# A gated linear recurrence taken in steps of 64 tokens in place of 128, ahead of two expert layers

## The chip, the cores and the metric

The kernel runs on one core of one Trainium2 chip. The metric is device time in microseconds (us), the median of several executions. A profile is one execution taken by the hardware profiler, and its times run from the start of its span. The engines are PE (TensorE, the matrix engine; its weight loads are listed apart as PEld and overlap the matmuls), DVE (VectorE), ACT (ScalarE), POOL (GpSimd) and SP (SyncE, which issues the transfers here).

## What is computed

A recurrence over 768 tokens for 4 batches of 8 heads with 48 features each, then two layers of the same size on its 3072 tokens by 384 features:

```python
def _attn_ref(q, k, v, f_logit):
    f = 1.0 / (1.0 + np.exp(-f_logit))
    state = np.zeros((B, H, D, D), dtype=np.float32)
    for t in range(S):
        state = f[:, :, t, :, None] * state + np.einsum('bhd,bhe->bhde', k[:, :, t], v[:, :, t])
        y[:, :, t] = np.einsum('bhd,bhde->bhe', q[:, :, t], state)
    return y

x = y.transpose(0, 2, 1, 3).reshape(B * S, H * D)
h = x @ w_in;  x = (h * clip(h + 3, 0, 6) / 6) @ w_out           # 384 -> 2048 -> 384
h = x @ w_in2; x = (h * tanh(log1p(exp(h)))) @ w_out2            # 384 -> 2048 -> 384
```

## The kernel before

**The recurrence in units.** A unit u is 128 tokens (C) of one batch, all 8 heads; there are 24, six to a batch, so units 0, 6, 12 and 18 begin a batch (`first`) and units 5, 11, 17 and 23 end one (`last`). Heads lie in four pairs p, two heads on 112 of the 128 rows (rows 0 to 47 and 64 to 111). `attention` (line 231) does for each unit: DVE bounds f (L245), ACT takes exp and log, DVE sums the logs along the tokens with one scan (L251; a `cap` tile with a zero at the first token of each pair starts each sum anew), ACT takes two exponentials, and DVE multiplies k and q by them (L201), so that the decay inside a unit has become a scale of each token. On PE then stand five pieces, all in f32: `scores` (L262), q times k for 128 by 128 tokens into two banks; `turn` (L281), four transposes of k, copied by ACT to `kn`; `outer` (L288), k outer v, which is what the unit adds to the state; and `values` (L302), q times the old state `sd` and then the masked scores A times v. DVE masks the two banks of scores (L271), adds the outer products to the state `st` and scales it (`carry`, L322 and L323), ACT copies the state into the two diagonal blocks of `sd` for the next unit, and ACT and DVE take the result apart into a high and a low half, `xh` and `xl` (L182, L198), which the layers multiply. A unit that ends a batch has no `turn`, `outer` and `carry`; one that begins a batch has no product with the state.

**The array in tiles.** A matmul that uses few rows or columns of the array is placed on a part of it, and parts work at the same time: in `scores` a matmul uses 48 rows and 128 columns (two parts), in `outer` 128 rows and 64 columns (two parts), in `values` 128 rows and 32 columns (four parts). An f32 matmul stands in the trace as two records, each with a weight load of its own; one of the layers' matmuls (f32r) is one record.

**The layers.** The weights of each layer stand in 16 slices f. The tokens go in blocks (384 or 512 tokens, the last of 256), seven to each layer. For each f of each block `hidden` (line 342) issues nine matmuls into a bank h (three parts of the features, times xh·wh, xl·wh, xh·wl), ACT and DVE form g and its halves gh and gl, and nine more matmuls add to three banks o. The first layer's weights are taken apart into `wh` and `wl` while block 0 runs: a transfer `raw`, two steps on ACT, two on DVE (L215, L217), one more of each (L182, L198).

**What sets the order.** `Plan` holds every operation with an engine, an estimated cost, the keys that it reads and writes, and a rank, and `emit` (line 110) lays the program out as a list scheduler: an engine that comes free takes the ready operation of the lowest rank. Every engine then runs its list in that order and waits where something isn't there. Units 0 to 3 stand at the head with ranks 1.1 apart (HEAD_GAP), ahead of block 0; the later ones are spread over the f of the block before theirs. Before rank 1, where PE would idle by the plan, `warm` puts filler matmuls on the tile `cap`, up to 30 us by the plan.

## Time and profile before

| what | us |
| --- | --- |
| median of 3 executions (lowest, highest) | 927.75 (927.59, 930.64) |
| the profiled execution itself | 927.91 |
| its span | 926.1 |
| PE busy | 907.6 (98%) |
| DVE busy | 673.6 (73%) |
| ACT busy | 571.2 (62%) |

The span is 1.8 us shorter than the time of the same execution. The three stretches that matter below are the head (0 to 34 us, units 0 to 3 and the first weights), block 0 (34 to 124.5 us) and all behind it. A row of instructions says at which us the first of a group began, how long the group took to its end (ends overlap, so paces are read from one start to the next), the engine, the line, the operation, what it writes and reads, and in brackets what the engine waited for.

### The profile page before, as it was taken

To read this page: it belongs to the slowest core of one execution; us is meant where nothing else is said; L and a number is where in the kernel's file an instruction comes from. 1 tells how busy PE (TensorE), PEld (TensorE's weight loads), DVE (VectorE), ACT (ScalarE), POOL (GpSimd) and SP (SyncE) were. 2 spreads that over 40 slices of the span, in tenths; PEclk is the share of its full clock that TensorE was granted. 3 is DMA by queue.
4 is the path that set the end of the run, shared out by engine and by line. 5 is a ranking of instruction groups with operands and counts; after the bars stand their busy time and mean duration, and the time that the engine had idled before them with its cause. 6 is when DMAs were issued, how large, how long until landed. Compare 5 with 4: busy or idle time off the path is not lost.

```text
span 926.1 us, 15491 instructions
## 1 busy us (share of the span) xinstructions
PE 907.6 (98%) x6173; PEld 799.3 (86%) x6173; DVE 673.6 (73%) x1127; ACT 571.2 (62%) x1022; POOL 0.2 (0%) x4
## 2 busy tenths in 40 slices
PE   9999899999999999999999999999999999999996
PEld 8777689999999988888899988888888888999996
DVE  7999876776555644453355887978878878888895
ACT  7889866666554544343255765766666666676674
POOL 0000000000000000000000000000000000000000
PEclk9999999999999999999999999999999999999998
DMA  9665466665321311110033300200100101000000
GB/s 275 214 211 179 156 218 209 197 216 195 114 65 52 99 42 42 43 46 2 1 103 120 126 21 0 69 1 8 56 0 18 43 1 33 23 7 27 1 27 21
DMA packets 33488, 75.92 MB, mean 82 GB/s; under 512 B 3840, under 2 KB 11008, under 8 KB 33408
## 3 DMA queue, kind: packets, MB, share of 16 engines
q1 hardware_dynamic: 33408, 74.86, 25.1%
q8 instruction: 50, 0.82, 0.4%
q14 instruction: 30, 0.25, 0.1%
HBM read 59.11 MB, written 15.73 MB: 81 GB/s over the span
## 4 chain that ended last, share of the span: by engine, by line
PE 84%; DVE 7%; DMA 3%; ACT 3%; issue 2%; SPq 0%; DVEq 0%; ACTq 0%
PE o L195 40%; PE h L195 26%; PE a L195 13%; PE m L195 5%; DMA raw<-w 2%; DVE we L215 1%; DVE we L217 1%; DVE wl L198 1%; DMA o<-ft 1%; DVE A L271 1%; DVE g L370 1%; ACT f L182 1%; DVE q L201 0%; PE m L283 0%; DMA f<-ft 0%
## 5 line engine op out<-in xcount | busy, mean ns | idle before, releaser
L195 PE MATMUL o<-gh,wh 128*128 128x512 f32 (+2 forms) x666 | 242.2, 364 | 0.0
L195 PE MATMUL o<-gh,wl 128*128 128x512 f32 (+2 forms) x666 | 239.3, 359 | 0.0
L195 PE MATMUL o<-gl,wh 128*128 128x512 f32 (+2 forms) x666 | 239.2, 359 | 0.0
L195 PE MATMUL h<-xh,wh 128*128 128x384 f32 (+2 forms) x471 | 172.1, 365 | 1.1 <-ACT wh L182 0.8
L195 PE MATMUL h<-xh,wl 128*128 128x384 f32 (+2 forms) x471 | 169.7, 360 | 2.5 <-DVE wl L198 2.5
L195 PE MATMUL h<-xl,wh 128*128 128x384 f32 (+2 forms) x471 | 169.0, 359 | 0.3 <-DVE xl L198 0.3
L195 PEld LDWEIGHTS o<-gh,wh 128*128 128x128 f32 x666 | 125.2, 188 | 17.1 <-issue 2.4
L370 DVE SCALAR_TENSOR_TENSOR g<-g,h 128x384 f32<-128x384 f32 (+1 forms) x112 | 68.1, 608 | 97.6 <-ACT g L182 97.6
L195 PEld LDWEIGHTS o<-gh,wl 128*128 128x128 f32 x666 | 125.2, 188 | 13.2
L195 PEld LDWEIGHTS o<-gl,wh 128*128 128x128 f32 x666 | 125.3, 188 | 13.0 <-DVE gl L198 0.2
L182 ACT ACTIVATE g<-h,small 128x384 f32<-128x384 f32 (+1 forms) x112 | 69.7, 623 | 92.8 <-PE h L195 72.5
L182 ACT ACTIVATE gh<-q 128x512 fp32r<-128x512 f32 (+2 forms) x110 | 63.0, 573 | 86.5 <-DVE q L201 81.3
L195 PEld LDWEIGHTS h<-xh,wl 128*128 128x128 f32 x471 | 88.5, 188 | 14.3 <-DVE wl L198 5.5
L195 PEld LDWEIGHTS h<-xh,wh 128*128 128x128 f32 x471 | 88.5, 188 | 13.5 <-ACT wh L182 3.0
L182 ACT ACTIVATE gh<-g 128x384 fp32r<-128x384 f32 (+1 forms) x112 | 63.4, 566 | 56.6 <-DVE g L370 56.2
L195 PEld LDWEIGHTS h<-xl,wh 128*128 128x128 f32 x471 | 88.5, 188 | 8.9 <-DVE xl L198 0.7
L198 DVE TENSOR_TENSOR gl<-g,gh 128x384 fp32r<-128x384 f32 (+1 forms) x112 | 68.4, 611 | 35.7 <-ACT gh L182 35.6
L182 ACT ACTIVATE q<-k,small 128x512 f32<-128x512 f32 (+2 forms) x112 | 73.7, 658 | 14.4 <-DVE k L378 14.1
L201 DVE TENSOR_TENSOR q<-q,k 128x512 f32<-128x512 f32 (+2 forms) x112 | 68.6, 612 | 17.4 <-ACT q L182 16.2
L182 ACT ACTIVATE k<-k 128x512 f32<-128x512 f32 (+2 forms) x112 | 62.4, 562 | 20.5 <-DVE k L375 20.2
L198 DVE TENSOR_TENSOR gl<-q,gh 128x512 fp32r<-128x512 f32 (+2 forms) x110 | 67.3, 613 | 6.5 <-ACT gh L182 6.1
L378 DVE SCALAR_TENSOR_TENSOR k<-k 128x512 f32<-128x512 f32 (+2 forms) x112 | 67.7, 609 | 1.2 <-ACT k L182 0.9
(120 smaller groups left out, 1204.8 us busy)
## 6 DMA issues: line engine op xcount, KB each, us to landing
raw<-w SPq DMA_DIRECT2D x32, 768.0 KB, 4.6
v<-vn SPq DMA_DIRECT2D x24, 256.0 KB, 3.2
w<-we SPq DMA_DIRECT2D x16, 384.0 KB, 2.6
raw<-w SPq DMA_DIRECT2D x16, 384.0 KB, 3.0
k<-kt SPq DMA_DIRECT2D x23, 224.0 KB, 2.9
q<-qt SPq DMA_DIRECT2D x23, 224.0 KB, 3.3
f<-ft SPq DMA_DIRECT2D x22, 224.0 KB, 2.8
out_dram<-o SPq DMA_DIRECT2D x12, 256.0 KB, 2.0
```

Source lines behind the costliest of these rows:

```text
L182: lambda: nc.scalar.activation(out=out(), in_=in_(), func=func, **k), r, w)
L195: nc.tensor.matmul(**k)
L198: dve(n, rank, lambda: nc.vector.tensor_tensor(out=out(), in0=a(), in1=b().bitcast(F32), op=ALU.subtract), r, w)
L201: dve(n, rank, lambda: nc.vector.tensor_tensor(out=out(), in0=a(), in1=b(), op=ALU.mult), r, w)
L215: dve(768, rank, lambda: stt(out=eu(), in0=eu(), scalar=3, in1=v(0), op0=ALU.logical_shift_left, op1=ALU.bitwise_or), (e, raw, (raw, 0)), ...
L217: dve(768, rank, lambda: stt(out=eu(), in0=v(1), scalar=0x80000000, in1=eu(), op0=ALU.bitwise_and, op1=ALU.bitwise_or), (e, raw), (e,))
L271: nc.vector.tensor_tensor(out=A[i](), in0=zs[i]().rearrange("p (a c) -> p a c", a=4), in1=tri.unsqueeze(1).to_broadcast([128, 4, C]), op=A ...
L370: dve(n, rank, lambda: nc.vector.scalar_tensor_tensor(out=gg(), in0=gg(), scalar=6.0, in1=zn(), op0=ALU.min, op1=ALU.mult), (g, z), (g,))
L378: dve(n, rank, lambda: nc.vector.scalar_tensor_tensor(out=ee(), in0=ee(), scalar=2.0, in1=ee(), op0=ALU.add, op1=ALU.mult), (e,), (e,))
```

## The change

The unit stays 128 tokens, and its transfers, scan and multiplies of k and q stay, but the recurrence inside goes in two halves c of 64 tokens (CC). The log sums start anew every 64 tokens. `scores` multiplies each half with itself only: 16 matmuls of 48 rows and 64 columns on four parts of the array, in place of 8 on two; the masks are 256 columns wide in place of 512. `outer` is called twice, once for each half: `outer(0)` on rows 0 to 63 of kn with parts of 64 by 64, now in one operation with `scores` and ahead of it, `outer(1)` on rows 64 to 127 with parts of 64 by 32, now at the start of `values`. `values` has 32 matmuls of 64 columns for A times v on eight parts (16 of 128 columns on four before) and 24 of 64 columns for q times the state (12 of 128 before; 12 in a unit that begins a batch, 0 before), and now takes A before the state. `carry` and the copies to `sd` run twice a unit, with a second `sd`; the unit that ends a batch does `turn`, `outer(0)` and one `carry` too. xh and xl are made in two halves. The planner's costs and ranks of these operations are set anew (0.5, 1.0 and 1.7 us for `turn`, `scores` and `values`; before 0.5, 1.1, 1.7, and 0.9 for `outer`), and units 1 and 3 no longer borrow other tiles for A.

```diff
-C = 128
+C, CC = 128, 64
...
-    sd = const.tile([R, NP, PD], F32, name="sd")
+    sd = [const.tile([R, NP, PD], F32, name=f"sd{c}") for c in range(2)]
...
-        A = [new(nm, [128, 4, C], bufs) for nm, bufs in (
-            (("gl", 3), ("gl", 3)) if early and u == 1 else (("gl", 3), ("g", 1)) if third else (("A", 2), ("A", 2)))]
-        head = lambda p, i: A[i]()[:, p]
+        A = new("A", [128, 512], 2)
+        Av = lambda: A().rearrange("p (i a c) -> p i a c", i=2, a=NP)
+        zt = bank("m", [128, 512], 1)
+        kn = new("kn", [128, NP, R], 1)
+        ztv = lambda: zt()[:, 0:NP * R].rearrange("p (a b) -> p a b", a=NP)
+
+        def turn():
+            for p in range(NP):
+                nc.tensor.transpose(ztv()[:, p, :], k3()[:, p, :], ident[0:R, 0:R])
+
+        pe(0.5, rk(3), turn, (k, "ident"), (zt,))
+        act(448, rk(4), lambda: flat(kn()), lambda: flat(ztv()), AF.Copy, (zt,), (kn,))
+
         zs = [bank("a", [128, 512], 2) for i in range(2)]
+        steps = range(1 if last else 2)
+        zu = [bank("o0" if early else "m", [128, 512], 1) for c in steps]
+        zuv = [lambda z=z: z()[:, 0:NP * D].rearrange("p (a b) -> p a b", a=NP) for z in zu]
+
+        def outer(c, w):
+            t = slice(c * CC, c * CC + CC)
+            for p in range(NP):
+                for g in range(0, R, w):
+                    to = slice(g, min(g + w, R))
+                    at = p * 128 + (0 if g < HB else 128 - D)
+                    mm(out=zuv[c]()[to, p, :], lhsT=kn()[t, p, to], rhs=v()[t, at:at + D], start=True, stop=True)
 
         def scores():
+            outer(0, HB)
             for p in range(NP):
-                for i, (r0, r1) in enumerate(SPANS):
-                    mm(out=zs[i]()[:, p * C:(p + 1) * C], lhsT=k3()[r0:r1, p, :], rhs=q3()[r0:r1, p, :], start=True,
-                       stop=True)
-
-        pe(1.1, rk(4), scores, (k, q), zs)
+                for c in range(2):
+                    for i, (r0, r1) in enumerate(SPANS):
+                        t = slice(c * CC, c * CC + CC)
+                        mm(out=zs[i]()[t, p * CC:(p + 1) * CC], lhsT=k3()[r0:r1, p, t], rhs=q3()[r0:r1, p, t],
+                           start=True, stop=True)
+
+        pe(1.0, rk(5), scores, (k, q, kn, v), (*zs, zu[0]))
         for i in range(2):
             def mask(i=i):
-                nc.vector.tensor_tensor(out=A[i](), in0=zs[i]().rearrange("p (a c) -> p a c", a=4),
-                                        in1=tri.unsqueeze(1).to_broadcast([128, 4, C]), op=ALU.mult)
-
-            dve(512, rk(5 + i), mask, (zs[i], "tri"), (A[i],))
-        if not last:
-            zt, zu = bank("m", [128, 512], 1), bank("o0" if early else "m", [128, 512], 1)
-            kn = new("kn", [128, NP, R], 1)
-            ztv = lambda: zt()[:, 0:NP * R].rearrange("p (a b) -> p a b", a=NP)
-            zuv = lambda: zu()[:, 0:NP * D].rearrange("p (a b) -> p a b", a=NP)
-
-            def turn():
-                for p in range(NP):
-                    nc.tensor.transpose(ztv()[:, p, :], k3()[:, p, :], ident[0:R, 0:R])
-
-            pe(0.5, rk(5), turn, (k, "ident"), (zt,))
-            act(448, rk(6), lambda: flat(kn()), lambda: flat(ztv()), AF.Copy, (zt,), (kn,))
-
-            def outer():
-                for p in range(NP):
-                    for i, (r0, r1) in enumerate(((0, HB), (HB, R))):
-                        at = p * 128 + (0, 128 - D)[i]
-                        mm(out=zuv()[r0:r1, p, :], lhsT=kn()[:, p, r0:r1], rhs=v()[:, at:at + D],
-                           start=True, stop=True)
-
-            pe(0.9, rk(7), outer, (kn, v), (zu,))
-        zx = bank("h" if early else "a", [128, 512], 2)
-        zxv = lambda: zx()[:, 0:KC * C].rearrange("p (a b) -> p a b", a=KC)
-
-        def strip(n):
-            return zxv()[n % 4 * 32:n % 4 * 32 + 32, n // 4, :]
+                nc.vector.tensor_tensor(out=Av()[:, i], in0=zs[i]()[:, 0:NP * CC].rearrange("p (a c) -> p a c", a=NP),
+                                        in1=tri[:, 0:CC].unsqueeze(1).to_broadcast([128, NP, CC]), op=ALU.mult)
+
+            dve(256, rk(6), mask, (zs[i], "tri"), ((A, i),))
+        def update(c):
+            def carry():
+                fv = b()[:, :, c * CC + CC - 1:c * CC + CC].to_broadcast([R, NP, D])
+                if first and not c:
+                    nc.vector.tensor_tensor(out=st, in0=zuv[c]()[0:R], in1=fv, op=ALU.mult)
+                else:
+                    nc.vector.tensor_tensor(out=st, in0=st, in1=zuv[c]()[0:R], op=ALU.add)
+                    nc.vector.tensor_tensor(out=st, in0=st, in1=fv, op=ALU.mult)
+
+            P.op("dve", 0.27 if first and not c else 0.54, rk(6.5 + c), carry, (zu[c], b, "st"), ("st",))
+            for i, (r0, r1) in enumerate(SPANS):
+                act(192, rk(7 + c), lambda r0=r0, r1=r1, i=i, c=c: sd[1 - c][r0:r1, :, i * D:i * D + D],
+                    lambda r0=r0, r1=r1: st[r0:r1], AF.Copy, ("st",), (("sd", 1 - c, i),))
+        update(0)
+        zx = [bank("h" if early else "a", [128, 512], 2) for c in range(2)]
+        zxv = [lambda z=z: z()[:, 0:KC * CC].rearrange("p (a b) -> p a b", a=KC) for z in zx]
+
+        def strip(n, c):
+            return zxv[c]()[n % 4 * 32:n % 4 * 32 + 32, n // 4, :]
 
         def values():
-            if not first:
-                for n in range(3 * NP):
-                    p, j = divmod(n, 3)
-                    mm(out=strip(n), lhsT=sd[:, p, j * 32:j * 32 + 32], rhs=q3()[:, p, :], start=(n < 4), stop=False,
-                       skip_group_check=True)
+            if not last:
+                outer(1, 32)
             for w in range(2):
                 for n in range(w, 3 * NP, 1 + 2 * w):
                     p, j = divmod(n, 3)
                     at, i = ((0, 0), (32, 0), (96, 1))[j] if not w else (64, 1)
-                    mm(out=strip(n), lhsT=v()[:, p * 128 + at:p * 128 + at + 32], rhs=head(p, i),
-                       start=(first and not w and n < 4), stop=(j != 1 or w == 1), skip_group_check=True)
-
-        pe(1.0 if first else 1.7, rk(7), values, (v, *A, q, ("sd", 0), ("sd", 1)), (zx,))
+                    for c in range(2):
+                        t = slice(c * CC, c * CC + CC)
+                        mm(out=strip(n, c), lhsT=v()[t, p * 128 + at:p * 128 + at + 32], rhs=Av()[t, i, p, :],
+                           start=(not w and n < 4), stop=(j != 1 or w == 1) and first and not c, skip_group_check=True)
+            for c in range(first, 2):
+                for n in range(3 * NP):
+                    p, j = divmod(n, 3)
+                    mm(out=strip(n, c), lhsT=sd[c][:, p, j * 32:j * 32 + 32], rhs=q3()[:, p, c * CC:c * CC + CC],
+                       start=False, stop=True, skip_group_check=True)
+
+        pe(1.3 if first else 1.7, rk(8), values,
+           (v, kn, (A, 0), (A, 1), q, *(("sd", c, i) for c in range(first, 2) for i in range(2))), (*zx, *zu[1:]))
         if not last:
-            def carry():
-                fv = b()[:, :, C - 1:C].to_broadcast([R, NP, D])
-                if first:
-                    nc.vector.tensor_tensor(out=st, in0=zuv()[0:R], in1=fv, op=ALU.mult)
-                else:
-                    nc.vector.tensor_tensor(out=st, in0=st, in1=zuv()[0:R], op=ALU.add)
-                    nc.vector.tensor_tensor(out=st, in0=st, in1=fv, op=ALU.mult)
-
-            P.op("dve", 0.27 if first else 0.54, rk(8), carry, (zu, b, "st"), ("st",))
-            for i, (r0, r1) in enumerate(SPANS):
-                act(192, rk(9), lambda r0=r0, r1=r1, i=i: sd[r0:r1, :, i * D:i * D + D], lambda r0=r0, r1=r1: st[r0:r1], AF.Copy,
-                    ("st",), (("sd", i),))
+            update(1)
         o = u * C - BLOCKS[0][j][0]
         xs = X[1, j]
-        act(384, rk(8), lambda: xs[0]()[:, :, o:o + C], zxv, AF.Copy, (zx,), ((xs[0], o),))
-        sub(384, rk(8.5), lambda: xs[1]()[:, :, o:o + C], zxv, lambda: xs[0]()[:, :, o:o + C], (zx, (xs[0], o)),
-            ((xs[1], o),))
+        for c in range(2):
+            w = slice(o + c * CC, o + c * CC + CC)
+            act(192, rk(9), lambda c=c, w=w: xs[0]()[:, :, w], lambda c=c: zxv[c](), AF.Copy, (zx[c],), ((xs[0], w.start),))
+            sub(192, rk(9.5), lambda c=c, w=w: xs[1]()[:, :, w], lambda c=c: zxv[c](), lambda c=c, w=w: xs[0]()[:, :, w],
+                (zx[c], (xs[0], w.start)), ((xs[1], w.start),))
...
-        return [(X[ph, j][p], o) for o in (range(0, n, C) if ph == 1 else range(KC))]
+        return [(X[ph, j][p], o) for o in (range(0, n, CC) if ph == 1 else range(KC))]
...
-        nc.vector.memset(cap.rearrange("p (a b) -> p a b", a=NP)[:, :, 0:1], 0.0)
+        nc.vector.memset(cap.rearrange("p (a b) -> p a b", b=CC)[:, :, 0:1], 0.0)
...
-        "cst": np.stack([np.eye(128, dtype=np.float32), np.triu(np.ones((128, 128), np.float32))]),
+        "cst": np.stack([np.eye(128, dtype=np.float32), np.tile(np.triu(np.ones((CC, CC), np.float32)), (2, 2))]),
```

DVE at the head, the last of the operations up to the last `xl` of the four units of block 0, which the first matmuls on `xl` wait for (we and wl are weights, b and gh decays, st the state). Before:

```order
L245 TENSOR_SCALAR f<-f 112x512 x2
L198 TENSOR_TENSOR xl<-h,xh 128x3x128
L322 TENSOR_TENSOR st<-st,o_487 112x192
L323 TENSOR_TENSOR st<-st,gh 112x192
L251 SCALAR_TENSOR_TENSOR b<-cap,f 112x512
L215 SCALAR_TENSOR_TENSOR we<-we,raw 128x768
L217 SCALAR_TENSOR_TENSOR we<-raw,we 128x768
L198 TENSOR_TENSOR xl<-h,xh 128x3x128
```

After, the same place:

```order
L201 TENSOR_TENSOR k<-k,f 112x512
L295 TENSOR_TENSOR A<-a,tri 128x256 x2
L305 TENSOR_TENSOR st<-st,o_743 112x192
L306 TENSOR_TENSOR st<-st,gh 112x192
L198 TENSOR_TENSOR wl_103<-we,wh_102 128x768
L201 TENSOR_TENSOR q<-q,b 112x512
L245 TENSOR_SCALAR f<-f 112x512
L215 SCALAR_TENSOR_TENSOR we<-we,raw 128x768
L305 TENSOR_TENSOR st<-st,o_788 112x192
L306 TENSOR_TENSOR st<-st,gh 112x192
L217 SCALAR_TENSOR_TENSOR we<-raw,we 128x768
L198 TENSOR_TENSOR xl<-h,xh 128x3x64 x2
```

The last `xl` is DVE's operation 43 in the list of before and stands at place 62 in that of after, with five and eleven operations on weights ahead of it.

PE in a steady unit in the second block, from the scores to the values (m is the bank of the transposes and outer products, a those of scores and values). Before:

```order
L195 MATMUL a<-q,k 128x128 x8
L195 MATMUL o_2908<-gh,wh_101 128x384
...
L283 MATMUL m<-ident,k 128x112 x4
L195 MATMUL h<-xh,wh_105 128x384
...
L195 MATMUL m<-v,kn 64x48
L195 MATMUL m<-v,kn 48x48
...
L195 MATMUL a<-q,sd 32x128 x12
L195 MATMUL a<-A,v 32x128 x16
```

After:

```order
L195 MATMUL m<-v,kn 64x48
L195 MATMUL m<-v,kn 48x48
...
L195 MATMUL a<-q,k 64x64 x16
L195 MATMUL o_3767<-gh,wh_110 128x384
...
L195 MATMUL h<-xh,wh_114 128x384
...
L195 MATMUL m<-v,kn 32x48 x3
L195 MATMUL m<-v,kn 16x48
...
L195 MATMUL a<-A,v 32x64 x32
L195 MATMUL a<-q,sd_96 32x64 x12
L195 MATMUL a<-q,sd_97 32x64 x12
```

The outer products of the first half have moved ahead of the scores, those of the second half behind the layers' matmuls and ahead of A times v, and the products with the state behind it.

## Rows read from the trace of the kernel before

**Rows 1.** The page: busy time, share of the span, instructions of each engine.

```profile
PE 907.6 (98%) x6173; PEld 799.3 (86%) x6173; DVE 673.6 (73%) x1127; ACT 571.2 (62%) x1022; POOL 0.2 (0%) x4
```

**Rows 2.** Windows: stretch, length; busy PE, PEld, DVE, ACT, POOL; PEclk, DMA, GB/s.

```profile
0.00:34.00 34.00, 31.24 (x453) 27.86 (x453) 27.39 (x48) 24.21 (x46) 0.20 (x4) 1.00 0.91 264
34.00:104.00 70.00, 64.58 (x560) 50.29 (x561) 68.42 (x99) 60.88 (x104) 0.00 (x0) 1.00 0.57 189
104.00:124.50 20.50, 18.88 (x75) 13.16 (x74) 16.80 (x22) 16.41 (x24) 0.00 (x0) 1.00 0.45 154
124.50:260.60 136.10, 136.00 (x1118) 128.62 (x1116) 93.16 (x153) 84.53 (x153) 0.00 (x0) 1.00 0.56 189
```

**Rows 3.** Instructions of the tile wl: shortest, median, longest ns; first and last start.

```profile
L198 DVE TENSOR_TENSOR wl<-we,wh x16: 931/951/959, 26.7 to 119.8; 128x768 fp32r<-128x768 f32 x16
```

**Rows 4.** The chain that ended last: a run of 384 columns, one of 512.

```profile
272.70 3.12 PE h L195 x18
...
384.31 2.04 PE h L195 x9
```

**Rows 5.** Timeline of PE over one steady unit in the second block.

```profile
260.63 1.16 PE L195 MATMUL a<-q,k 48*128 48x128 f32 x16
261.73 0.45 PE L195 MATMUL o<-gh,wh 128*128 128x384 f32 x1
...
263.40 0.55 PE L283 MATMUL m<-ident,k 112*128 112x112 f32 x4
263.72 0.42 PE L195 MATMUL h<-xh,wh 128*128 128x384 f32 x1
...
265.49 0.67 PE L195 MATMUL m<-v,kn 128*64 128x48 f32 x16
266.08 0.86 PE L195 MATMUL a<-q,sd 112*32 112x128 f32 x24
266.76 1.06 PE L195 MATMUL a<-A,v 128*32 128x128 f32 x32
267.75 0.44 PE L195 MATMUL o<-gh,wh 128*128 128x384 f32 x1
...
277.31 1.16 PE L195 MATMUL a<-q,k 48*128 48x128 f32 x16
```

**Rows 6.** Groups by line and shape, weight loads: busy us, mean ns, idle before.

```profile
L195 PEld LDWEIGHTS a<-q,k 48*128 48x128 f32 x368 | 23.5, 187 | 7.9 <-issue 4.7 <-DVE q L201 1.4 <-DVE A L271 0.6
...
L195 PEld LDWEIGHTS m<-v,kn 128*64 128x64 f32 x128 | 8.6, 137 | 7.0 <-issue 3.3 <-ACT kn L182 3.1 <-ACT raw L182 0.4
...
L195 PEld LDWEIGHTS a<-A,v 128*32 128x32 f32 x640 | 17.7, 110 | 0.7 <-DVE st L320 0.4 <-issue 0.2
```

**Rows 7.** Groups by line and shape, DVE and ACT.

```profile
L251 DVE TENSOR_TENSOR_SCAN b<-cap,f 112x512 f32<-112x512 f32 x22 | 26.8, 1220 | 1.5 <-ACT f L182 1.2
...
L201 DVE TENSOR_TENSOR k<-k,f 112x512 f32<-112x512 f32 x22 | 15.1, 686 | 2.8 <-ACT f L182 2.8
...
L182 ACT ACTIVATE sd<-st 48x192 f32<-48x192 f32 x40 | 14.2, 356 | 0.3
...
L201 DVE TENSOR_TENSOR q<-q,k 128x256 f32<-128x256 f32 x16 | 6.8, 423 | 1.0 <-ACT q L182 0.8
...
L323 DVE TENSOR_TENSOR st<-st,b 112x192 f32<-112x192 f32 x14 | 5.0, 358 | 0.5
```

**Rows 8.** Timeline of DVE and of PE, the end of the head.

```profile
33.41 0.55 DVE L198 TENSOR_TENSOR xl<-h,xh 128x384 fp32r<-128x384 f32 x1
...
34.02 0.50 PE L195 MATMUL h<-xl,wh 128*128 128x512 f32 x1 [0.34 <-DVE xl L198]
```

**Rows 9.** Windows and timelines of PE: around one stop within the values.

```profile
24.00:30.00 6.00, 5.46 (x133) 4.51 (x133) 5.55 (x12) 3.71 (x8) 0.00 (x0) 1.00 1.04 292
...
27.49 0.15 PEld L195 LDWEIGHTS h<-A,v 128*32 128x32 f32 x5 [0.81 <-issue]
...
27.49 0.31 PE L195 MATMUL h<-A,v 128*32 128x128 f32 x3 [0.54 <-issue]
```

More of the change, by code (lines that the diff above doesn't have):

```diff
@@ L415, in fast_path @@
     dma(CST_RANK + 0.5, lambda: ident, lambda: cst[0], (), ("ident",), 65536)
-    P.op("dve", 0.5, -100, lambda: nc.vector.memset(sd, 0.0), (), ("st", ("sd", 0), ("sd", 1)))
+    P.op("dve", 0.5, -100, lambda: [nc.vector.memset(x, 0.0) for x in sd], (),
+         ("st", *(("sd", c, i) for c in range(2) for i in range(2))))
     zw = bank("o1", [128, 512], 1)
```

## The prediction

> **What bounds the kernel now.** The page comes first [rows 1]: PE is busy for 98% of the span, DVE for 73%. The average hides that the stages differ, so the windows come next, which split the start by stage [rows 2]. In the head (0 to 34 us) PE is at work but on fillers and units 0 to 3, and what ends it is DVE: the first matmul on xl starts at 34.02, having waited for DVE's last xl [rows 8]. In block 0 DVE is busy for 68.42 of the 70 us from 34 to 104, since it takes the weights apart there; PE idles for 5.42 us in that window and for 1.62 in the next, 7.0 in all. The weights' last step starts at 119.8 [rows 3], and block 0 ends 4.7 us later. From 124.5 on PE is busy for 136.00 of 136.1 us and DVE for 93.16: PE alone decides. The granted clock is 1.00 in all four windows. So a microsecond less on PE counts behind 124.5; before that, it is DVE's list that decides.
>
> **A unit on PE, before.** From the scores at 260.63 to the next at 277.31 lie 16.68 us [rows 5] with 72 matmuls of 384 columns at 3.12/18 = 0.173 [rows 4], 12.48 us, so a unit costs 4.20: from start to start 1.10 for scores, 0.32 for the transposes, 0.59 for outer, 0.68 for q times the state, 0.99 for A times v, and some 0.5 that the layers' first matmuls lose beside them. By round of the array: scores have 16 records on two parts, 8 rounds; loads of 128, 64 and 32 columns take 187, 137 and 110 ns [rows 6], about 0.8 ns a column, so the 128-column load plus little else gives 8 x 0.112 = 0.90 and some 0.2 for changing how the array is divided. Outer has 8 rounds of 0.058 (64-column loads). Q times the state and A times v have 6 and 8 rounds of 0.109, the streaming of 128 columns. The rounds and the transposes give 3.2; the remaining 1.0 I put down to five changes of division at 0.2.
>
> **The same unit after.** Outer of the first half: 16 records of 64 columns on two parts at a time, 8 x 0.058 = 0.47. Scores: 32 records on four parts, 8 rounds, now with a 64-column load: 0.47. Outer of the second half: 32 records with 32-column loads on four parts, 8 x 0.042 = 0.34. A times v: 64 records on eight parts, 8 rounds of 64 streamed columns at half of 0.109: 0.445. Q times the state: 48 on four parts, 12 x 0.056 = 0.67. Transposes 0.32. Outer and scores share a division, and so do the second outer and A times v: five changes stay. Sum 2.71 + 1.0 = 3.71, against 4.20: 0.5 less (0.6 if a change costs less with narrower loads). A unit that begins a batch goes from 3.55 (no product with the state) to 3.38, one that ends it from 3.17 to 3.37, since it now has transposes and one outer. This assumes that eight parts take records at 0.007 us each, which no stretch of before sustains; its nearest rows stand below.
>
> **The head.** Units 0 to 3 must be through before the first h. On DVE, what stands ahead of block 0's last xl grew from 26.3 us of work to 36.2: the order puts eleven weight operations there in place of five, 6 x 0.87 = +5.2 (their starts are 0.87 to 0.97 apart, 0.95 alone [rows 3]), one scan more, +1.14 (1.22 alone [rows 7]), four multiplies of k or q, +2.4 (0.686 alone, 0.60 start to start), one bound of f, +0.34, seven carry operations more, +2.6 (0.358 an operation [rows 7]), xl in halves +0.3, the masks at half width -2.1. The chain of one unit is also longer: outer, carry, copy to sd, then values, with one kn and one bank for the outer products. DVE idled for some 7.5 us ahead of its xl at 33.41 [rows 8]; I take 2.5 more. 36.2 + 10 = 46.2, and the first h at **47 in place of 34**; 41 if the other engines' waits hide the weight work, 50 at the worst. Nothing is lost of the weight work itself: it is done early, and DVE's whole work ahead of the last weight is 104 us in place of 106.
>
> **Block 0.** 288 matmuls of 512 columns at 2.04/9 = 0.227 [rows 4] are 65.3 us. Before, 34.0 to 124.5 held them, attention of some 17 us (four units, and the transposes and outer products of two more) and 8 of waits and losses, 7.0 of them PE idle [rows 2]. After, less attention falls in there: unit 4 has its first half ahead of the first h (2.05 left), units 5, 6 and 7 are whole (3.37 + 3.38 + 3.71) and the transposes of unit 8 (0.3): 12.8. The weights are ahead by then, so of the waits I keep 2.4. 47 + 65.3 + 12.8 + 2.4 = 127.5, **+3.0**. From DVE's side the last weight can't come much before 118 to 121 either way, which puts the end at 123 or later.
>
> **Behind block 0.** Before: 11 regular units, two that begin and three that end a batch, less two units' transposes and outer products already done: 46.2 + 7.1 + 9.5 - 1.9 = 60.9. After: 40.8 + 6.8 + 10.1 - 0.3 = 57.4. The gain is 3.5, or 4.6 with cheaper changes; I take **-4.1**.
>
> **What the second update costs.** Per unit DVE does two narrow masks less half each (-0.53; 0.423 is the nearest price of 256 columns [rows 7]) and two more carry steps (+0.66), ACT two more copies to sd (0.356 each). The new chain is outer, carry, copy, product with the state, inside one unit: two masks 0.85, two carry steps 0.7, two copies 0.7, and hand-overs, 2.5 to 3.7 with a queue on DVE. Between scores and values the order has 18 to 36 matmuls of the layers in every unit from 4 on (one has 99), 3.1 us at the least, with the second outer and A times v behind them 3.9. So I cost it at nothing; where the cover fails it is up to 1 us a unit.
>
> **Sum.** +3.0 in block 0 and -4.1 behind it: -1.1 against the profiled 927.91, **926.8 us**. That execution lies 0.16 above the median of 927.75.
>
> **Rivals.** *The head hides more.* If the first h starts by 42, PE again waits for weights, and DVE's list sets block 0's end: 2 us less work on it, last weight at 118, end at 122.5. That is -2.0 and -4.1 to -4.6 behind it: about 921.5. For it: DVE's idle time in the head; against it: the xl that the first h waits for stands behind all that weight work.
>
> *The instruction supply runs dry (slower).* At 27.49 PE stopped within A times v for 0.54 us with nothing that it waited for, 0.81 in its weight loads, when the DMA engines were full (share 1.04) [rows 9]. There 144 instructions (a load and a matmul each record) came in 2.3 us. After, values is 288 in some 1.6 us. If each unit stops once for as long, 20 x 0.81 = 16 us: about 942; in every second unit, 935. It decides from the point where that burst uses up what lies ready. Against it: behind block 0 the DMA share is 0.56 and falling, and before never stopped there.
>
> *More parts don't take more records.* The fastest long run of records before is 24 in 0.68 us, 0.028 each (products with the state [rows 5]). If that is what PE can issue and not what four parts can stream, 192 records a unit take 5.4 + 0.32 + 1.0 = 6.8 us, 2.6 more than before: some 45 to 50 us in 19 units, about 975, and the change doesn't do what it says. Against it: after the stop at 27.49 three matmuls started within 20 ns of each other [rows 9], 0.007 to 0.010 each, on parts that stood free. The Trainium skill (TensorE: Matmul & The Clock Gate, section "Wait — 56ns, not 53.3ns?") states such a rule: from start to start a matmul never takes less than about 25 ns, however few its columns. The pace of 0.028 would agree with it, the three starts within 20 ns do not, and no row here shows a long run on eight parts; by that rule the time would be this rival's.
>
> **Chances and range.** The forecast (923 to 931) 0.45; the hidden head 0.22; the dry supply 0.21; no more records 0.12. About 0.5%, 4.6 us, is what a measurement of this kernel tells from no change: faster means under 923.1, slower over 932.4. Faster: most of the second case and a fifth of the first, 0.27. Same: the rest of the first and traces of the others, 0.41. Slower: the dry supply, the last case, and what the second chain may cost, 0.32. The range goes from 919.5 (DVE-set end, cheap changes) to 943 (a stop in every unit); the last rival is left out.
>
> **What will show it.** The first matmul on xl at about 47 and DVE without gaps ahead of it; block 0 ending at 127 to 128; a unit at 3.6 to 3.7 us of attention; values without "issue" waits. Wrong would be: scores or A times v whose time doesn't halve, stops named "issue" in values, PE waiting for sd or the carry in the units behind block 0, or a first h at 42 or earlier.

## The result, and the profile after

The changed kernel takes 935.32 us in the median of nine executions (932.12 to 940.02), beside 929.87 for the kernel before on the same chips: a ratio of 1.0067, 95% interval 1.0050 to 1.0085. It is slower by two thirds of a percent, where 926.8 us and no measurable change were forecast; 935.3 lies within the range of 919.5 to 943. The profiled execution took 936.72 us with a span of 934.9, against 927.91 and 926.1 before.

The page's first line and the windows of the changed kernel, cut at the first matmul of the layers and at the end of block 0 (the first matmul of the block behind it; columns as in [rows 2]):

```profile
PE 912.2 (98%) x8693; PEld 809.2 (87%) x8693; DVE 679.5 (73%) x1200; ACT 589.1 (63%) x1098; POOL 0.2 (0%) x4
...
0.00:52.10 52.10, 41.87 (x993) 38.55 (x993) 38.51 (x75) 38.11 (x76) 0.20 (x4) 0.91 0.76 219
52.10:134.10 82.00, 78.63 (x952) 62.47 (x951) 71.84 (x111) 66.96 (x117) 0.00 (x0) 0.97 0.52 169
134.10:934.90 800.80, 791.69 (x6752) 708.18 (x6750) 569.12 (x1016) 484.06 (x908) 0.00 (x0) 1.00 0.20 64
```

The same before, with the first matmul on xh in the timeline (that on xl began at 34.02 [rows 8]):

```profile
33.20 0.48 PE L195 MATMUL h<-xh,wh 128*128 128x512 f32 x1
...
33.20:124.50 91.30, 83.94 (x637) 63.63 (x636) 85.99 (x122) 78.06 (x129) 0.00 (x0) 1.00 0.54 180
...
124.50:926.10 801.60, 792.91 (x5089) 707.96 (x5087) 561.01 (x960) 469.68 (x851) 0.00 (x0) 1.00 0.19 63
```

The head lasts 52.1 us in place of 33.2: 18.9 us are lost there. Block 0 itself is shorter than before, 82.0 us against 91.3, and ends at 134.1 against 124.5: 9.6 us late. Behind it the kernel takes 800.8 us against 801.6: 0.8 us less. So the whole loss is made in the first 52 us. Half of it comes back within block 0, where PE now idles for 3.4 us in place of 7.4 and is busy for 5.3 less, and almost nothing behind it.

The head on PE in the timeline (start, length to the last end, engine, line, operation, what it waited for), with the first matmul of the block behind block 0 as the last row:

```profile
20.73 0.63 PE L195 MATMUL h<-A,v 64*32 64x64 f32 x36 [1.72 <-issue]
...
32.09 0.76 PE L195 MATMUL h<-q,sd 112*32 112x64 f32 x37 [1.42 <-issue]
...
41.31 0.43 PE L195 MATMUL h<-q,sd 112*32 112x64 f32 x16 [0.78 <-issue]
...
46.44 1.51 PE L195 MATMUL h<-kl,sd 112*32 112x64 f32 x48
50.19 0.98 PE L195 MATMUL m<-v,kn 64*64 64x48 f32 x15 [2.24 <-ACT kn L182]
...
52.09 0.79 PE L195 MATMUL h<-xh,wh 128*128 128x512 f32 x1
...
134.10 0.33 PE L195 MATMUL h<-xh,wh 128*128 128x384 f32 x1
```

Three times PE stopped within the values with nothing that it waited for, 3.9 us in all: the stop of [rows 9], which the prediction calls the dry supply, in three units out of four. The row at 46.44 takes 1.51 us for 48 products with the state; behind block 0 the same row takes 0.88. The windows of that stretch (the eighth column is the granted clock) say why:

```profile
44.00:46.00 2.00, 0.94 (x88) 0.92 (x90) 1.97 (x5) 0.79 (x3) 0.00 (x0) 1.00 0.92 259
46.00:48.00 2.00, 1.95 (x85) 1.54 (x62) 1.94 (x4) 1.66 (x3) 0.00 (x0) 0.52 0.78 265
48.00:50.00 2.00, 0.00 (x0) 0.00 (x0) 1.97 (x6) 1.62 (x4) 0.00 (x0) 0.50 0.34 118
50.00:52.00 2.00, 1.81 (x48) 1.78 (x48) 0.87 (x3) 1.95 (x5) 0.00 (x0) 0.50 0.67 138
```

From 46 to 56 us the granted clock was 0.50, the lower of its two levels, and so it was from 22.2 to 25.6, 1.5 us behind the stop that ended at 20.73; from 40 to 46 PE had been busy for 3.6 of 6 us only. The first 18 matmuls of block 0 then took 6.3 us in place of 4.1. Before the change the clock was 1.00 throughout [rows 2].

A steady unit behind block 0, to set beside [rows 5]:

```profile
141.53 0.60 PE L195 MATMUL m<-v,kn 64*64 64x48 f32 x15
...
142.03 0.64 PE L195 MATMUL a<-q,k 48*64 48x64 f32 x29
...
142.60 0.44 PE L195 MATMUL h<-xh,wh 128*128 128x384 f32 x1
...
147.49 0.45 PE L195 MATMUL m<-v,kn 64*32 64x48 f32 x24
...
147.84 0.84 PE L195 MATMUL a<-A,v 64*32 64x64 f32 x61
148.61 0.88 PE L195 MATMUL a<-q,sd 112*32 112x64 f32 x48
...
149.42 0.44 PE L195 MATMUL o<-gh,wh 128*128 128x384 f32 x1
...
151.09 0.55 PE L265 MATMUL m<-ident,k 112*128 112x112 f32 x4
151.41 0.42 PE L195 MATMUL h<-xh,wh 128*128 128x384 f32 x1
...
154.71 0.60 PE L195 MATMUL m<-v,kn 64*64 64x48 f32 x15
```

From 141.53 to 154.71 lie 13.18 us with 54 matmuls of the layers (9.36 us), so a unit costs 3.82, against 4.20 before and 3.71 forecast. From start to start: first outer product and scores 1.07, second outer and A times v 1.12, products with the state 0.81, transposes 0.32. No piece waits, and behind block 0 PE waited for nothing but 0.2 us for a g of the layers.

### The profile page after: what moved, and what is told of

It is laid out like the page before. It is cut to its first block, busy times and chain, and to the rows that moved or that the text cites. A ratio compares the mean times of both kernels' runs of the same rounds, so it can differ in the third digit from the quotient of the medians.

```text
span 934.9 us, 20681 instructions
## 1 busy us (share of the span) xinstructions
PE 912.2 (98%) x8693; PEld 809.2 (87%) x8693; DVE 679.5 (73%) x1200; ACT 589.1 (63%) x1098; POOL 0.2 (0%) x4
## 4 chain that ended last, share of the span: by engine, by line
PE 89%; DMA 4%; DVE 3%; ACT 2%; issue 1%; SPq 0%; ACTq 0%
PE o L195 42%; PE h L195 29%; PE a L195 12%; PE m L195 6%; DMA raw<-w 3%; PE m L265 1%; DMA v<-vn 1%; DMA q<-qt 1%; ACT raw L182 1%; DVE we L217 0%; DVE we L215 0%; ACT f L182 0%; DVE b L251 0%; ACT wh L182 0%; DMA out_dram<-o 0%
## 5 line engine op out<-in xcount | busy, mean ns | idle before, releaser
L195 PEld LDWEIGHTS h<-xh,wl 128*128 128x128 f32 x471 | 88.9, 189 | 12.0 <-DVE wl L198 3.1
L198 DVE TENSOR_TENSOR gl<-g,gh 128x384 fp32r<-128x384 f32 (+1 forms) x112 | 68.5, 611 | 36.2 <-ACT gh L182 36.2
```

Of the source, the lines that this page charges most:

```text
L195: nc.tensor.matmul(**k)
L198: dve(n, rank, lambda: nc.vector.tensor_tensor(out=out(), in0=a(), in1=b().bitcast(F32), op=ALU.subtract), r, w)
```

## The experiments

**The two halves of the program.** Each unit can be set to one step or two. In the first run units 0 to 3 go in one step, all others in two; in the second the other way round. Both carry a second `cap` and a second mask, so that each form of unit has its own.

```diff
+HALF = lambda u: u >= 4
...
+        if not HALF(u):
+            A = [new(nm, [128, 4, C], bufs) for nm, bufs in (
...
+            return
         A = new("A", [128, 512], 2)
```

> Units 0 to 3 go in one step of 128 tokens as before, all later units in two of 64. Theory A (the loss is made ahead of block 0: its first matmul came at 52.1 in place of 33.2 us): the first matmul on xh is back at about 33, block 0 ends near 124, and the gain of the later units shows: 925 to 927 us, 0.997 to 0.999 of the kernel before. Rival B (the units behind the head cost as much or more than before): the time stays near 935, a ratio of 1.005 or more.

> The other half: units 0 to 3 in two steps of 64, all later ones in one step of 128. Theory A: block 0 begins at about 52 and ends at about 134 as in the changed kernel, and the time is 936 to 939 us, a ratio of 1.008 to 1.011, above the changed kernel itself. Rival B: the ratio is within 0.3% of the kernel before.

The first measured 926.89 us, a ratio of 0.9982 (0.9971 to 0.9993); the second 936.85 us, 1.0084 (1.0061 to 1.0108), with its first matmul of the layers at 50.7. Theory A stands: the loss is made by units 0 to 3. The windows of the first run, cut at the same events:

```profile
0.00:34.27 34.27, 30.78 (x452) 27.33 (x453) 27.09 (x48) 23.98 (x46) 0.83 (x6) 1.00 0.93 264
34.27:122.80 88.53, 81.43 (x1005) 63.04 (x1004) 83.34 (x128) 78.55 (x134) 0.00 (x0) 0.98 0.56 183
122.80:924.90 802.10, 792.08 (x6752) 708.04 (x6750) 568.55 (x1014) 484.39 (x908) 0.00 (x0) 1.00 0.20 64
```

The head is back at 34.3. Block 0 takes 88.5 us, against 91.3 from 33.2 to 124.5 before, and the stretch behind it 802.1 against 801.6: what the half steps give in this run, two thousandths, they give within block 0, and nothing behind it.

**The weight work on DVE.** The step that the forecast of the head rests on. Here the weights' operations on DVE and ACT read the last xl, from the second slice on:

```diff
+            gate = ((X[1, 0][1], 384 + CC),)
             for f in range(NF):
-                key, src = stream(w1, f, f - W_AHEAD)
-                weight(f, f - W_AHEAD + 0.5, key, src)
+                key, src = stream(w1, f, f - W_AHEAD, gate if f > 1 else ())
+                weight(f, f - W_AHEAD + 0.5, key, src, gate if f > 0 else ())
```

> The changed kernel, but the work of DVE and ACT on the weights from the second slice on waits for the last xl of block 0, so that five weight operations of DVE stand ahead of it, as before the change, in place of eleven. Theory A1 (it is the weight work that stands ahead on DVE): the last xl comes 5 us earlier, the first matmul of the layers at 46 to 47 in place of 52, and the time falls by up to 4 us, less what block 0 then waits for weights. Theory A2 (it is PE's own stops for instructions and the lower clock, which DVE then waits for): the first matmul stays at 50 to 52, and block 0 is longer, since the weights come later: 936 to 940 us.

939.07 us, 1.0110 (1.0093 to 1.0127). The first matmul came at 51.2: A1 falls. The chain of waits (start, us, what) says what held it, and the tile wl what it cost:

```profile
28.33 2.50 issue
...
31.58 2.08 PE o L195 x12
...
36.31 4.82 PE o L195 x44
...
L198 DVE TENSOR_TENSOR wl<-we,wh x16: 930/956/959, 25.7 to 134.2; 128x768 fp32r<-128x768 f32 x16
```

In the changed kernel the same tile (first and last start), and the windows up to the end of the last xl, first of the changed kernel, then of this run:

```profile
L198 DVE TENSOR_TENSOR wl<-we,wh x16: 947/952/959, 28.0 to 129.3; 128x768 fp32r<-128x768 f32 x16
...
0.00:50.19 50.19, 39.96 (x944) 36.76 (x944) 37.73 (x74) 36.25 (x72) 0.20 (x4) 0.93 0.76 221
...
0.00:49.20 49.20, 41.63 (x944) 38.34 (x944) 33.21 (x68) 32.56 (x67) 0.20 (x4) 0.90 0.73 209
```

DVE has 4.5 us less to do ahead of its last xl (33.21 in place of 37.73), and the xl ends only 1.0 earlier: DVE idles for 16.0 us in place of 12.5. PE is the chain itself: a stop of 2.5 us, then fillers (`o`, 12 records in 2.08 us, which take 1.4 at the full clock), then more of them ahead of the next outer product (the row at 36.31). And the last step on the weights held back starts at 134.2 in place of 129.3; block 0 takes 87.8 us in place of 82.0.

**The fillers and the clock.** Three runs change `warm` alone: a quarter as many fillers, each of 512 columns; fillers in the plan's first 8 us only; fillers up to the first matmul of the layers.

```diff
-            mm(out=zw()[0:R, 0:C], lhsT=cap[:, 0:R], rhs=cap[:, 0:C], start=True, stop=True)
+            mm(out=zw()[0:R], lhsT=cap[:, 0:R], rhs=cap, start=True, stop=True)
...
-        P.emit("pe", WARM, 0.22, warm)
+        P.emit("pe", WARM, 0.88, warm)
```

```diff
-WARM = 30
+WARM = 8
```

```diff
-WARM = 30
+WARM = 60
```

> The changed kernel with fillers of 512 columns, a quarter as many, so that the fillers use up a quarter of the instructions. Theory A2 (the head's bursts outrun the supply of instructions, and the fillers take part of it): the three stops named issue in the head (1.72, 1.42 and 0.78 us) shrink to under 1 us in all, the first matmul of the layers comes at 47 to 49, and the time falls by 3 to 4 us. If the supply depends on the bursts alone, the stops stay at 3 to 4 us and the time within 1 us of the changed kernel.

> The changed kernel with fillers in the plan's first 8 us alone. Theory A3 (the fillers stand in PE's line: once PE has stopped for instructions, or runs at the lower clock, it is behind the plan, and fillers meant for idle time delay units 1 to 3): the scores of unit 1 come at about 22 in place of 25.9 us, the first matmul of the layers at 47 to 49, the time falls by 2 to 4 us even if the clock is lower for longer. Theory A4 (the chain of dependent steps on DVE and ACT sets the head, PE's delay is only copied from it): the first matmul stays within 1 us of 52, and the time within 1 us.

> The changed kernel with fillers up to the first matmul of the layers (the plan's limit at 60 us in place of 30), so that PE doesn't idle between 42 and 50 us. If PE's idling is what the lower clock follows, the granted clock is 1.00 from 46 to 56, and block 0 ends 2 to 3 us earlier (its first 18 matmuls take 4.2 in place of 6.3 us): 932 to 934 us. If fillers only delay the work behind them: 936 us or more.

Wide fillers: 935.68 us, 1.0069 (1.0052 to 1.0087), first matmul at 52.4. The stops of the head are 3.9 us as before, and two more of 1.4 us each stand in block 0, where the changed kernel has none: the bursts of the recurrence outrun the supply, not the fillers. Hardly any fillers: 933.75 us, 1.0055 (1.0034 to 1.0076), first matmul at 48.8, although PE's records up to 47 us take the time of the lower level (four transposes 1.01 us each time, 0.55 at the full clock); one stop of 1.7 us was left. The windows read a clock of 1.00 there all the same, since the first record of the clock in this trace begins at 46.9: here the level has to be read from the lengths of the instructions. The time lies between what the two theories expected. Its chain has no fillers. It alternates between the units' own steps on PE, at the lower level, and, from 34.7 on, the weight work and the scan:

```profile
34.68 0.94 DVE wl L198
...
36.83 1.14 DVE b L251
...
44.49 0.93 ACT we L182
...
47.29 0.44 ACT kn L182
```

Long fillers: 931.83 us, 1.0022 (1.0008 to 1.0035), 3.5 us under the changed kernel with an interval apart from its own, as expected if PE's idling is what the lower clock follows. Seven of its eight executions had a mean granted clock of 0.996 to 0.998 and took 929.1 to 933.1 us; the eighth, 0.991 and 936.55, is the one profiled (a stop of 2.9 us up to 31.5, lower level from 31 to 41 us, first matmul at 55.1). The changed kernel's nine had 0.987 to 0.994. So what the head looks like with the clock held is not in any trace.

**Both cuts at once.**

> Both cuts at once: the weight work from the second slice on waits for the last xl of block 0, and fillers stand in the plan's first 8 us alone. With the weights held back alone, PE's own line (fillers, stops for instructions, lower clock) led to the first matmul at 51.2; without fillers alone, DVE's and ACT's weight work led to it at 48.8. If these are two chains of nearly one length, either of which holds the first matmul, it comes at 42 to 46 now; if a third one holds it (the steps of one unit after the other), at 48 or later. The time stays above 930 us in either case, since the weights held back are then late in block 0, as they were at 939 us.

941.49 us, 1.0132 (1.0106 to 1.0159), first matmul at 49.8, not 42 to 46: a third chain, the steps of one unit after the other, is about as long as the other two. It is so at PE's lower level, at which four transposes take 1.01 us here too; how long it would be at the full clock, no run shows. The late weights cost what they cost before (block 0 takes 88.9 us).

**The units one after the other.** In PE's order of the kernel before, the scores of units 1 to 3 stand ahead of the values of the unit before each; A times v of units 0 to 3 begins at 16.0, 22.0, 25.9 and 29.7. In the changed kernel scores wait for kn, of which there is one, and A times v begins at 18.5, 29.5, 39.1 and 45.4. Four runs work on that. In two, both outer products stand beside the scores in the unused halves of the scores' two banks, and two states take turns (the second with long fillers too):

```diff
-        zu = [bank("o0" if early else "m", [128, 512], 1) for c in steps]
+        zu = zs
...
-            outer(0, HB)
+            for c in steps:
+                outer(c, HB)
...
+                    o, n = (st, st2) if not c else (st2, st)
+                    nc.vector.tensor_tensor(out=n, in0=o, in1=zuv[c]()[0:R], op=ALU.add)
+                    nc.vector.tensor_tensor(out=n, in0=n, in1=fv, op=ALU.mult)
```

> The changed kernel (all units in two steps of 64) with both outer products beside the scores and two states in turn, so that in the head the second outer product no longer waits for the first half's update, and kn and the bank come free earlier. Theory A4 (the chain of dependent steps sets the head: in the run without fillers PE waited 5.5 us for st and 3.9 for kn, and the first matmul came at 48.8 though PE ran at the lower clock to 47): the waits for st are gone, the first matmul comes at 44 to 48, block 0 ends at 126 to 129, the time is 927 to 931 us. If stops and the lower clock set it: still 50 to 53, and 933 to 935 us, less only what the units behind block 0 gain (2 to 3 us).

> The same with fillers up to the first matmul of the layers. The median with long fillers in the changed kernel was 3.5 us lower, with a mean granted clock of 0.996 in most runs in place of 0.990. If the lower clock costs that here too: 2 to 4 us under the run without long fillers. If the shorter chain leaves PE no idle time in the head, or fillers delay it: within 1 us of it.

934.13 us, 1.0057 (1.0040 to 1.0074), first matmul at 50.7; with long fillers 932.84 us, 1.0042 (1.0027 to 1.0056). The wait for st (1.7 us in the head of the changed kernel) is gone there, and the head is hardly shorter: PE now waits ahead of the scores, for kn.

```profile
PE a L197 <- ACT kn L184: 4.5, 2, 2.3
```

So the second outer product's wait was not what held the head. The long fillers bring 1.3 us here, less than the 2 to 4 expected, with intervals that overlap.

In the other two there are two kn; in the first of them scores also stand in an operation of their own:

```diff
-        kn = new("kn", [128, NP, R], 1)
+        kn = new("kn", [128, NP, R], 2)
```

```diff
+        pe(0.5, rk(5), lambda: outer(0, HB), (kn, v), (zu[0],))
+
         def scores():
-            outer(0, HB)
...
-        pe(1.0, rk(5), scores, (k, q, kn, v), (*zs, zu[0]))
+        pe(0.5, rk(4), scores, (k, q), zs)
```

> The changed kernel with scores in an operation of their own, which doesn't wait for kn, and two kn in place of one, so that units 0 to 3 can overlap on PE again, as they did before the change (the order of PE has the scores of a unit ahead of the values of the one before it, and half as many fillers). Theory A5 (scores tied to the one kn make each unit begin when the one before it has ended, and that series holds the head whatever else is cut): the first matmul of the layers comes at 42 to 46, the time is 928 to 932 us. If the length of one unit's own steps and the weight work between them hold it: 49 to 52 and 933 to 936 us.

> The same with the two kn alone, scores still in one operation with the first outer product. Theory A5: since scores wait for their own kn but no longer for the other unit's second outer product, most of the gain is there: first matmul at 44 to 48, 929 to 933 us. If it is the tie of scores to kn itself and not the single buffer: as the changed kernel, 50 to 52 and 934 to 936 us.

With scores on their own and two kn the first matmul comes at 44.9, 7 us earlier than in the changed kernel, the largest step of any run that keeps the half steps in the head:

```profile
37.54 0.69 PE L195 MATMUL a<-q,k 48*64 48x64 f32 x32
38.05 0.61 PE L195 MATMUL o<-v,kn 64*64 64x48 f32 x16
...
44.91 0.76 PE L195 MATMUL h<-xh,wh 128*128 128x512 f32 x1 [1.58 <-ACT we L182]
```

With two kn alone it stays at 51.8, and there it is DVE's last xl that it waits for:

```profile
51.80 0.63 PE L195 MATMUL h<-xh,wh 128*128 128x512 f32 x1 [3.73 <-DVE xl L198]
```

So the tie of scores to kn holds some 7 of the 19 us, and the single buffer by itself nothing. Two things are not separated: no run has scores on their own with one kn, and in the run at 44.9 the stops for instructions came to 1.3 us in place of 3.9, which may be part of the 7. Yet the times don't show it: 935.19 us, 1.0062 (1.0042 to 1.0082), and 936.87, 1.0079 (1.0053 to 1.0105). In the first of the two, block 0 ended at 130.1, 4 us earlier, but the stretch behind it took 3.8 us longer than in the changed kernel: summed from start to start, scores and outer product apart cost 1.3 us in themselves, and 2.7 were lost among the layers' matmuls.

**The pace on eight parts.**

```diff
-            for w in range(2):
+            for w in (0, 1, 1, 1, 1, 1):
...
+                        nn = CC // 2 if w else CC
+                        mm(out=strip(n, c)[:, 0:nn], lhsT=v()[t, p * 128 + at:p * 128 + at + 32], rhs=Av()[t, i, p, 0:nn],
```

> The changed kernel, in which the last eight matmuls of A times v are made with 32 columns in place of 64, and made five times over; the sums are then not those of the recurrence, and the time isn't to be compared. It measures the pace on eight parts: A times v took 0.0100 us a record (64 in 0.63 us) where 0.007 was forecast. If streaming 64 columns on each part sets it, or the weight load beside it, the 80 narrow records go at 0.006 to 0.008; if it is how fast PE takes records, at 0.010 still.

This kernel leaves out half the columns of its last products A times v, and only paces are read from it. Two units in the timeline, and the wait that this kernel has most of:

```profile
156.44 1.35 PE L195 MATMUL a<-A,v 64*32 64x64 f32 x125
...
161.07 0.27 PE L195 MATMUL a<-q,sd 112*32 112x64 f32 x2 [2.48 <-issue]
...
174.44 1.17 PE L195 MATMUL a<-A,v 64*32 64x64 f32 x104
177.15 0.32 PE L195 MATMUL a<-A,v 64*32 64x32 f32 x21 [1.53 <-issue]
...
PE a L195 <- issue: 19.8, 10, 3.5
```

Started without a stop between them, the narrow records of a unit go at 0.0091 us each. Those of 64 columns go at 0.0105: in the steady unit above, 0.63 us lie from the first start to the last of the 61 records of its row at 147.84. Halving the columns takes an eighth off. So it isn't the streaming that sets the pace, nor the load of 32 columns: in the second outer product a part takes such a load and 48 columns every 0.043 us (24 records on four parts from 147.49 to 147.74), which on eight parts would be 0.0054 a record. What is left, by elimination and not by a run of its own, is the rate at which PE gets its records; behind the stop at 177.15, where some lay ready, the 21 narrow ones went at 0.0063. And with values of 416 instructions PE stops for up to 3.5 us, ten times on the bank of scores and values, where values of 288 stopped in the head of the changed kernel but never behind its block 0.

**A version that beats both.** Units 0 to 3 and those that end a batch in one step, the rest in two, with both outer products beside the scores and two states:

```diff
+HALF = lambda u: u >= 4 and u % 6 != 5
```

> Meant to beat both kernels. Units 0 to 3 and the units that end a batch go in one step of 128, the others in two of 64, with both outer products beside the scores on four parts (they stand in the unused half of the two banks of scores) and two states that take turns. By the trace: 48 to 64 records at 0.0152 make outer products and scores 1.4 us together, in place of 1.07 and 0.38 with a change of division saved ahead of A times v: 0.1 to 0.3 us less in each of 13 units, 0.2 less in each of 4; 923 to 926 us, 0.994 to 0.997. If the second update, now ahead of the values, comes too late for them, PE waits for sd behind block 0: 927 us or more.

> As the version that beat both (both outer products beside the scores, units that end a batch in one step), but units 4 to 6, whose preparation falls into block 0, where DVE is the busiest engine, go in one step of 128 too. If the half steps pay only behind block 0: 924 to 926 us, the same as with units from 4 on. If block 0 gains from the shorter work on PE: 926 to 928 us.

925.08 us, 0.9953 (0.9935 to 0.9970): faster than both. With units 4 to 6 in one step too, 926.79 us, 0.9981 (0.9970 to 0.9992), as expected if block 0 gains from the half steps. Its trace doesn't show that gain in block 0. The windows of block 0, first of the better version, then of this one:

```profile
33.98:124.04 90.06, 83.09 (x869) 62.54 (x868) 82.99 (x123) 76.93 (x130) 0.00 (x0) 0.98 0.54 180
...
35.62:125.73 90.11, 83.67 (x690) 63.07 (x691) 82.91 (x118) 76.01 (x126) 0.00 (x0) 0.98 0.54 179
```

Block 0 is equally long, and of the 2.3 us between the two profiled executions 1.6 lie ahead of it (the first matmul at 35.6 in place of 34.0). Whether that comes of unit 4's form or is chance, one trace of each doesn't tell. A unit of the better version:

```profile
251.38 0.77 PE L201 MATMUL a<-v,kn 64*64 64x48 f32 x27
...
252.11 0.69 PE L201 MATMUL a<-q,k 48*64 48x64 f32 x28
...
259.20 0.86 PE L201 MATMUL a<-A,v 64*32 64x64 f32 x64
259.99 0.88 PE L201 MATMUL a<-q,sd 112*32 112x64 f32 x48
```

Both outer products (27 records in the first row, 5 more among the scores) and the scores take 1.35 us together, as the mean of 13 units, in place of 1.07 and 0.35, and the values follow with 0.79 and 0.81.

## Why the prediction was wrong

The forecast of 926.8 was a sum of three terms: a head of 47 us with block 0 ending 3.0 late, and -4.1 behind it. The profiled execution lies 9.9 above it: 5.1 in the head, 1.5 in block 0, 3.3 behind.

**The head (52.1 against 47), the step that failed.** The prediction worked it out as DVE's list: 36.2 us of work ahead of the last xl and 10 of idle time. The work was nearly right (37.7), the idle time was 12.5 (before, up to the end of the last xl, the windows have 6.6 of it and not 7.5). What fails is the statement that DVE's order sets the head: with 4.5 us of the weight work held back, DVE idled for 16.0, and the first matmul stayed at 51.2. The profile had shown that units overlapped on PE before, and the diff that scores now read kn; I counted that as 2.5 us of longer chain, and the run with scores on their own and two kn puts it at some 7. Not in the sum for the head were that stops for instructions (3.9 us, which I had only as a rival for every unit) push PE behind its plan, so that fillers meant for idle time delay work, and that the clock fell twice behind stretches in which PE idled. The long fillers, with which the mean clock was up in seven executions of eight and the median fell by 3.5 us, put the last at some 3 us, an estimate. Weight work, PE's line and a unit's own steps are three chains within 3 us of each other, the last as measured at the lower level: cutting one leaves the next. How the 19 us divide beyond the 7 isn't settled.

**Block 0 (82.0 against 80.5).** Right in kind: the waits fell, as the weights were ahead at first. PE idled for 3.4 us, not 2.4, and the layers' matmuls took 66.3 us in place of 65.3, since the lower clock took 2.2 from the first 18 (6.3 in place of 4.1); attention took 12.3, not 12.8. The 65.3 was itself misread: up to the next block's first matmul the trace has 270 of the 288 matmuls, before and after the change, and the losses beside them made up for it. That the weights would stay ahead was wrong: their last step moved from 119.8 to 129.3, since DVE's list has them between the layers' operations and moves with PE.

**Behind block 0 (-0.8 against -4.1).** The mechanism was right, the sizes were not. A regular unit gained 0.38, not 0.49 or 0.6, since A times v went at 0.0105 us a record on eight parts, where 0.007 was taken from three starts behind a stop [rows 9], a burst and not a pace: 11 units, 1.2 us. Another 0.6 I had added for cheaper changes of division. The units that begin a batch gained nothing in place of 0.17 each, 0.3 in all. Some 1.2 us are left. Summed from start to start over the whole stretch, the recurrence takes 51.5 us on PE in place of 53.0, and the layers' matmuls 740.2 in place of 739.7, where the windows of one unit each had them 0.04 cheaper a unit: that is most of what is left. No row names a cause for it, and it stays open.

**What held.** Scores on four parts take about half (0.51 us from 37.54 to 38.05 in the run with scores on their own, 1.10 before); the second update costs PE nothing behind block 0, where no row waits for sd or st; a unit that ends a batch is dearer (which the better version uses). Of the rivals, the dry supply came, but in the head only, three stops in all, and not once behind block 0, so in this kernel values of 288 instructions between the layers' matmuls are under the point from which it decides and values of 416 over it. That rival named 935 us for a stop in every second unit: the agreement with 935.3 is chance, as is that the time lies in a range whose upper end stood for a stop in every unit. That more parts take no more records is wrong as put, at 0.028 a record: the trace has 0.0105. The Trainium skill's rule (TensorE: Matmul & The Clock Gate, section "Wait — 56ns, not 53.3ns?") of about 25 ns from start to start doesn't hold for records on different parts of the array here; a pace at which PE takes records exists, but it is 9 to 11 ns.

## What to carry to other kernels

A change that is priced in the steady state must be followed through the head apart: there each unit's steps stand in a row, and one new dependence (scores on kn, some 7 us) took more than the 0.8 us that all behind block 0 gave back. Dense bursts of small matmuls can be held by the supply of instructions and not only by columns: take the pace of small matmuls from a long run of them, never from the few that start behind a stop. And where several chains of like length end at one event, cutting one of them shows little; put the old form back in that stretch alone, as the run with units 0 to 3 in one step did, before looking for the cause within it.

## What the runs showed of the hardware

PE's instructions come in pieces of 16 KB: the trace of the changed kernel has 70 such transfers on one queue for PE's 17,386 matmuls and weight loads, some 250 each. The three stops of its head stand behind PE's records 222, 477 and 732, 255 records (510 instructions, two pieces) apart, and with the weight work held back or with long fillers the stops stand behind records 222 and 477 as well, at other times: a stop falls where a piece ends. The transfers that the three stops waited for begin at 18.2, 29.5 and 38.7 us and last 1.1; PE resumed at 20.73, 32.09 and 41.31, 2.5 to 2.6 us behind each beginning. A burst that uses up what lies ready before the next piece has come stops, whether or not the DMA engines are full: their share was 1.03 around the first stop and 0.25 to 0.65 around the second. The length of a burst alone doesn't decide: single stops stood behind block 0 in two other runs, 0.4 us with both outer products beside the scores and 1.4 us with units 4 to 6 in one step. On eight parts PE took a record in 0.0091 to 0.0105 us, on four with 64 streamed columns in 0.014. Changing the division of the array cost the layers' matmul next to it some 0.1 us on either side (0.28 in place of 0.17 from 149.42, 0.26 from 151.41, 0.27 for the one that ends at 147.49), as it did before the change.
